# A fused state-space and gated-MLP layer: the state projection uses four PSUM banks in turn instead of two

## The chip, the core and the metric

The kernel runs on one NeuronCore of a Trainium2 chip. The core has five engines that run side by side, each through its own program in order, and wait for one another by semaphores: TensorE (PE in the profile; PEld is its weight load), VectorE (DVE), ScalarE (ACT), GpSimdE (POOL) and SyncE (SP), which here only issues DMAs. TensorE writes its products to PSUM, of which this kernel uses eight buffers ("banks") of 128 partitions by 512 float32 numbers. The metric is the time of one execution on the device in microseconds (us), the median over several runs.

## The reference

x has 2048 rows of 512 numbers. It is normalised (layer norm) to xn, and the output is x + A(xn) + B(xn):

```python
xn = _layernorm(x, axis=-1)
# A: a diagonal complex state-space layer with 512 states
Bu = jnp.einsum("bld,pd->blp", x + 0j, B_bar)
for t in range(L):
    h = Lam_bar[None, :] * h + Bu[:, t, :]
y = 2.0 * jnp.einsum("blp,dp->bld", hseq, Cmat).real + x * Dskip[None, None, :]
# B: a gated MLP with 1792 hidden units
h = _silu(gate) * up
out = jnp.einsum("bsf,fd->bsd", h, w2)
```

Here `x` inside A and B is xn. The state projection is the `Bu` product, in its real and its imaginary part; the factor that turns B into B_bar is applied elsewhere in the kernel (it is folded into C).

## The kernel before

The 2048 rows are cut into four blocks b = 0 to 3 of 512 rows (`TBLK`), and each block has these stages.

**Layer norm** gives `xn` (rows on partitions) and its transpose `xnT`. Block 0 is transposed on TensorE, the others by DMA. Block 1 is normalised by VectorE, blocks 2 and 3 by ScalarE (L269 sums, L275 squares, L285 the result); for block 3 the unneeded elementwise result of L269 and L275 goes to buffers of the `y_ps` pool.

**Gated MLP** (`glu(b)`, L512): for each of 14 slices f of 128 hidden units, four matmuls with w1 and four with w3 (L518, 128x512 each) fill two banks of the `gu_ps` pool, ScalarE reads them out with Silu (L527) and Copy (L528), and VectorE multiplies the two for pairs of slices (L536) into `act`.

**State projection** (`bu(b)`, L425): for two halves hf, two tiles j in a half and the real and imaginary part ri, eight groups of four matmuls each (L434). This text numbers the groups of a block 1 to 8. Each group accumulates in one bank, and ScalarE copies the bank to the tile `u` (L436, "eviction"). `u` has three buffers, one per half. A bank can be written again when its eviction is done, and a buffer of `u` when VectorE has finished with its former content. `bu(b)` stands inside `glu(b)` before slice 8, 8 and 4 for b = 0, 1, 2 (`AHEAD`), and for b = 3 it stands by itself after `glu(2)`.

**Scan** (`ssm_tasks(b)`, L442): VectorE rotates `u` (L456, L459, L463), runs eight scans along time (L473), rotates back (L479, L483), and GpSimdE issues a DMA that adds the last part into `act` (L487).

**Output product** (`y_fast(n)`, L701, n = 0 to 7, two for each block): a 256-row pair times the stacked weights in seven half-size products instead of eight (`mms`, L717, 128x256 matmuls). VectorE forms the sums of input tiles (L676, L759) and of results (L728), and ScalarE copies partial results from bank to bank (L737) and seeds banks (L698). The four result banks come from `gu_ps` or from two of `bu_ps` and two of `y_ps` (`seeds`, L682: `bu_ps` and `y_ps` for n = 0, 3, 4 and 6). The pair's rows are stored from `xn`.

PSUM has three pools: `ps_gu` with four banks, `ps_bu` with two and `ps_y` with two; a pool hands out its banks in turn. The order of work on each engine is written out by hand (`manual_schedule`): the code's order is the order of the engine's program. VectorE's work of the scan and of the weight sums is placed between the other work by `Filler` (L23), which counts assumed costs, not times that it measures: `bg.tensor(0.86)` after each projection group, for instance. Small ScalarE tasks (`sins`) are placed by `sin_step`, one at a time.

Around the later part of the kernel the order on TensorE is `y_fast(1)`, `glu(2)` with `bu(2)` in it, `bu(3)`, `y_fast(2)`, `y_fast(3)`, `glu(3)`, `y_fast(4)` to `y_fast(7)`.

Of the kernel before, what the change touches and what calls it, by code (L numbers as in the profile page):

```python
# [14 lines left out]
FP32 = DT.float32  # L15
BF16 = DT.bfloat16
FP16 = DT.float16
P = 128
# [45 lines left out]
def kernel(  # L64
# [22 lines left out]
    TBLK = CPB * P  # L87
# [31 lines left out]
    ps_bu = ctx.enter_context(tc.tile_pool(name="ps_bu", bufs=2, space=bass.MemoryType.PSUM))  # L119
    ps_y = ctx.enter_context(tc.tile_pool(name="ps_y", bufs=2, space=bass.MemoryType.PSUM))  # L120
# [214 lines left out]
    def sin_step(until=None):  # L335
        while sins and (until is None or until not in sins_done):
            key, fn = sins.popleft()
            fn()
            sins_done.add(key)
            if until is None:  # L340
                break
# [83 lines left out]
    def bu(b):  # L425
        for hf in range(NPT // 2):
            u = up.tile([P, 2, 2, TBLK], BF16, name="u")
            u_blk[b, hf] = u
            for j in range(2):
                pt = 2 * hf + j  # L430
                for ri in range(2):
                    ps = ps_bu.tile([P, TBLK], FP32, name="bu_ps")
                    for dt in range(NDT):
                        nc.tensor.matmul(out=ps, lhsT=bt[:, ri, dt, pt * P:(pt + 1) * P], rhs=xnT_blk[b][:, dt, :],  # L434
                                         start=(dt == 0), stop=(dt == NDT - 1))
                    nc.scalar.activation(out=u[:, j, ri, :], in_=ps, func=ACT.Copy)  # L436
                    bg.tensor(0.86)
                if (b == 0 and pt > 0) or (b == 1 and ri == 1) or (b == 2 and pt > 1):
                    sin_step()
            bg.fill()  # L440
# [71 lines left out]
    def glu(b):  # L512
# [77 lines left out]
        for f in range(f0, NFT):  # L590
            if f == AHEAD[b]:
                if b == 0:
                    ssm_tasks(0)
                bu(b)
            g_ps = ps_gu.tile([P, TBLK], FP32, name="gu_ps")
            mms(g_ps, w1_sb, f, slice(0, TBLK))
            u_ps = ps_gu.tile([P, TBLK], FP32, name="gu_ps")
            mms(u_ps, w3_sb, f, slice(0, TBLK))
            evac(f, g_ps, u_ps)
            if b in (1, NBLK - 1) and f == NFT - 3:  # L600
                seeds(0 if b == 1 else 4)
            if b == 0 and f == FIRST:
                sin_step((0, 0))
            elif b > 0 or f != MID - 1:
                sin_step()
            bg.tensor(1.72)
            bg.fill()
            if pend and f % 2 == 0:
                gate()
# [227 lines left out]
    sin_step(("ln", 3, True))  # L837
    seeds(2)
    bu(3)
    res_tasks(2)  # L840
    posts = ssm_tasks(3, True)
# [44 lines left out]
```

## Time and profile before

| | |
|---|---|
| median of 5 runs | 206.68 us (206.41 to 207.63) |
| the profiled execution's own time | 206.41 us |
| its span, from first to last instruction | 204.6 us |
| TensorE, matmul busy | 198.0 us (97%) |
| VectorE busy | 179.0 us (87%) |
| ScalarE busy | 125.1 us (61%) |
| GpSimdE busy | 35.0 us (17%) |
| projection matmuls (L434), 124 records | 28.9 us |
| projection evictions (L436), 32 | 18.8 us, 594 ns each |

A matmul's record lasts longer than its turn on the engine, because matmuls are pipelined: a 128x512 matmul is shown with 379 ns, but one starts every 216 ns (111 records fill the 24.00 us from 144 to 168). A wait shorter than the difference leaves no idle time in the record, and must be found from the starts. About one matmul record in fifty is missing from the trace. In lists of instructions in order of time, the columns are start, duration, engine, line, operation, tiles written and read, shapes, count, and in brackets the idle time before and what ended it. In the chain that ended last they are start, duration, and engine, tile and line.

### The profile page before, as it was taken

Reading aid. Unit: us, or ns where it says so; the run is one execution under the profiler, and the core shown is the slowest. Engines: PE = TensorE matmul, PEld = TensorE weight load, DVE = VectorE, ACT = ScalarE, POOL = GpSimd, SP = SyncE. Lnnn points to the kernel's source line nnn. Section 1 sums busy time; section 2 is a strip of 40 time slices with the busy share of each in tenths; the row PEclk is TensorE's granted clock in tenths of the full one; section 3 lists DMA queues with packets and bytes.
Section 4 is the critical chain, followed back from the end, with each engine's and each line's share of the span. In section 5 each row is a group of like instructions: output and inputs, shape, how many; then the busy total and the mean of one; then the engine's idle time right before and its main releaser. Section 6 shows DMA issues by size and latency. Waiting matters only on the chain.

```text
span 204.6 us, 3425 instructions
## 1 busy us (share of the span) xinstructions
PE 198.0 (97%) x1304; PEld 122.2 (60%) x1317; DVE 179.0 (87%) x248; ACT 125.1 (61%) x251; POOL 35.0 (17%) x59
## 2 busy tenths in 40 slices
PE   7999999999999999999999999999999999999994
PEld 2864444444444578854444444888444458888893
DVE  3789699999987999999969999997999998857932
ACT  4799788699999956689767775210566672101010
POOL 3250289500310040231010001011000011100000
PEclk9999999999999999999999999999999999999999
DMA  6899999993870002414660003219200037151011
GB/s 172 258 225 185 316 187 109 352 221 112 154 144 13 0 0 54 103 51 79 106 128 0 0 0 65 42 39 205 68 0 0 0 74 135 35 122 51 29 40 38
DMA packets 27832, 20.01 MB, mean 98 GB/s; under 512 B 15912, under 2 KB 26280, under 8 KB 27816
## 3 DMA queue, kind: packets, MB, share of 16 engines
q1 hardware_dynamic: 25512, 13.21, 28.1%
q0 software_dynamic: 1728, 6.29, 16.3%
q10 hardware_dynamic: 576, 0.30, 0.5%
q8 instruction: 10, 0.16, 0.4%
q14 instruction: 6, 0.05, 0.1%
HBM read 7.74 MB, written 2.10 MB: 48 GB/s over the span
## 4 chain that ended last, share of the span: by engine, by line
PE 45%; DVE 41%; ACT 5%; issue 4%; DMA 4%; POOL 1%; ACTq 0%; DVEq 0%
PE gu_ps L518 15%; PE gu_ps L717 11%; DVE u L473 7%; PE y_ps L717 7%; PE bu_ps L717 6%; DVE act L536 5%; PE bu_ps L434 4%; DVE p L456 3%; DVE u L459 3%; DMA xn<-x_blk 3%; DVE tw L655 2%; DVE u L463 2%; DVE stats L214 2%; DVE act L483 2%; DVE xn L728 2%
## 5 line engine op out<-in xcount | busy, mean ns | idle before, releaser
L518 PE MATMUL gu_ps<-xnT,w_sb 128*128 128x512 bf16 x415 | 92.0, 379 | 0.5
L518 PEld LDWEIGHTS <-w_sb 128*128 128x128 bf16 x424 | 41.4, 98 | 49.6 <-issue 0.3
L717 PEld LDWEIGHTS <-act 128*128 128x128 f16 x451 | 43.2, 98 | 6.3 <-DVE act L759 0.9
L527 ACT ACTIVATE g<-gu_ps 128x512 bf16<-128x512 f32 x55 | 33.0, 601 | 13.7 <-PE gu_ps L518 13.1
L528 ACT ACTIVATE u<-gu_ps 128x512 bf16<-128x512 f32 x55 | 33.2, 603 | 9.6 <-PE gu_ps L518 9.2
L434 PE MATMUL bu_ps<-xnT,bt 128*128 128x512 bf16 x124 | 28.9, 379 | 0.9 <-ACT u L436 0.4
L434 PEld LDWEIGHTS <-bt 128*128 128x128 bf16 x128 | 12.5, 98 | 16.7 <-issue 2.1
L436 ACT ACTIVATE u<-bu_ps 128x512 bf16<-128x512 f32 x32 | 18.8, 594 | 5.9 <-PE bu_ps L434 4.9
L473 DVE TENSOR_TENSOR_SCAN u<-rho,act,u 128x512 bf16<-128x512 f32 x16 | 19.5, 1265 | 0.0
L536 DVE TENSOR_TENSOR act<-g,u 128x1024 f16<-128x1024 bf16 x28 | 19.0, 678 | 0.3 <-ACT u L528 0.3
L487 POOL DMA_DIRECT2D act<-p x8 | 7.2, 898 | 65.3 <-DVE act L483 43.6
L456 DVE TENSOR_TENSOR p<-u,tabe 128x2048 bf16<-128x2048 bf16 x8 | 9.8, 1219 | 1.8 <-ACT g L527 1.6
L717 PE MATMUL y_ps<-tw,act 128*128 128x256 f16 x88 | 10.9, 273 | 0.0
L717 PE MATMUL gu_ps<-w_sb,act 128*128 128x256 bf16 (+1 forms) x84 | 10.8, 268 | 0.0
L717 PE MATMUL gu_ps<-tw,act 128*128 128x256 f16 x88 | 10.8, 273 | 0.0
L737 ACT ACTIVATE bu_ps<-y_ps 128x256 f32<-128x256 f32 x4 | 1.5, 369 | 13.7 <-PE y_ps L717 13.7
L459 DVE TENSOR_TENSOR u<-u,tabe 128x2048 bf16<-128x2048 bf16 x8 | 9.8, 1219 | 0.1
L479 DVE TENSOR_TENSOR p<-u,tabe 128x2048 f16<-128x2048 bf16 x8 | 9.8, 1220 | 0.1
L473 DVE TENSOR_TENSOR_SCAN u<-rho,ends,u 128x512 bf16<-128x512 f32 x8 | 9.8, 1264 | 0.0
L463 DVE TENSOR_TENSOR u<-u,p 128x2048 bf16<-128x2048 bf16 x8 | 9.7, 1216 | 0.1
L483 DVE TENSOR_TENSOR act<-u,tabe 128x2048 f16<-128x2048 bf16 x8 | 9.7, 1214 | 0.0
L717 PEld LDWEIGHTS <-tw 128*128 128x128 f16 x99 | 8.8, 98 | 0.9
(140 smaller groups left out, 253.7 us busy)
## 6 DMA issues: line engine op xcount, KB each, us to landing
act<-p POOLq DMA_DIRECT2D x8, 512.0 KB, 5.1
xn<-x_blk POOLq DMA_DIRECT2D x4, 512.0 KB, 5.6
out_dram<-xn SPq DMA_DIRECT2D x15, 128.0 KB, 1.7
w_sb<-in_B_w_dram SPq DMA_DIRECT2D x1, 1792.0 KB
x_blk<-in_A_x_dram SPq DMA_DIRECT2D x3, 512.0 KB, 11.8
w_sb<-in_B_w_dram SPq DMA_DIRECT2D x2, 768.0 KB, 7.3
w_sb<-in_B_w_dram SPq DMA_DIRECT2D x4, 256.0 KB, 3.7
w_sb<-in_B_w_dram SPq DMA_DIRECT2D x2, 512.0 KB, 7.1
```

What stands on the lines that cost most here:

```text
L434: nc.tensor.matmul(out=ps, lhsT=bt[:, ri, dt, pt * P:(pt + 1) * P], rhs=xnT_blk[b][:, dt, :], start=(dt == 0), stop=(dt == NDT - 1))
L436: nc.scalar.activation(out=u[:, j, ri, :], in_=ps, func=ACT.Copy)
L456: nc.vector.tensor_tensor(out=st["p"], in0=st["g"], in1=tabe[:, psl, 1:3, :], op=ALU.mult)
L459: nc.vector.tensor_tensor(out=st["g"], in0=st["g"], in1=tabe[:, psl, 0:1, :].to_broadcast(FULL), op=ALU.mult)
L463: nc.vector.tensor_tensor(out=st["g"], in0=st["g"], in1=st["p"][:, :, ::-1, :], op=ALU.subtract)
L473: nc.vector.tensor_tensor_scan(out=v, data0=rho[:, pt:pt + 1].to_broadcast([P, TBLK]), data1=v, initial=init, op0=ALU.mult, op1=ALU.add)
L483: nc.vector.tensor_tensor(out=act_state(b, hf), in0=st["g"], in1=tabe[:, psl, 0:1, :].to_broadcast(FULL), op=ALU.mult)
L518: nc.tensor.matmul(out=ps[:, tsl], lhsT=w[:, dt, f * P:(f + 1) * P], rhs=xnT[:, dt, tsl], start=(dt == 0), stop=(dt == NDT - 1))
L527: nc.scalar.activation(out=g16[:, f % 2, :], in_=g_ps, func=ACT.Silu)
L528: nc.scalar.activation(out=u16[:, f % 2, :], in_=u_ps, func=ACT.Copy)
L536: nc.vector.tensor_tensor(out=act(b)[:, k0:k1 + 1:k1 - k0, :], in0=g16, in1=u16, op=ALU.mult)
L717: nc.tensor.matmul(out=out, lhsT=left[:, k, :], rhs=right[k][:, cols], start=(start and k == 0), stop=(k == NK - 1), skip_group_check=True)
```

## The change

Of the eight projection groups of a block, those with j = 0 (groups 1, 2, 5, 6) still take a bank from `ps_bu`, and those with j = 1 (groups 3, 4, 7, 8) take one from `ps_y`. A group therefore reuses the bank of the group four before it, not two before it. Matmuls, evictions, assumed costs and the order of every engine's instructions are what they were. The lines after the first edited one move down by one.

```diff
             for j in range(2):
                 pt = 2 * hf + j
                 for ri in range(2):
-                    ps = ps_bu.tile([P, TBLK], FP32, name="bu_ps")
+                    pool, name = (ps_bu, "bu_ps") if j == 0 else (ps_y, "y_ps")
+                    ps = pool.tile([P, TBLK], FP32, name=name)
                     for dt in range(NDT):
                         nc.tensor.matmul(out=ps, lhsT=bt[:, ri, dt, pt * P:(pt + 1) * P], rhs=xnT_blk[b][:, dt, :],
                                          start=(dt == 0), stop=(dt == NDT - 1))
```

## The prediction

> **What bounds the kernel now.** I read the busy shares first, then the chain that ended last, then TensorE's waits, then the four projection stages in order of time. The busy shares name TensorE:
>
> ```profile
> PE 198.0 (97%) x1304; PEld 122.2 (60%) x1317; DVE 179.0 (87%) x248; ACT 125.1 (61%) x251; POOL 35.0 (17%) x59
> ```
>
> Busy matmul records overlap, so the share says where to look, not what is free. The chain says where TensorE sets the end:
>
> ```profile
> 89.29 0.34 DVE xn L728
> ...
> 95.65 0.70 ACT xn L285
> 96.34 0.50 ACT u L436
> 96.84 0.04 issue
> 96.88 2.53 PE bu_ps L434 x11
> ...
> 123.22 1.15 DVE act L483
> 124.37 0.02 issue
> 124.39 0.02 ACTq L436
> 124.41 0.04 issue
> 124.45 0.61 ACT u L436
> 125.06 0.04 issue
> 125.10 1.89 PE bu_ps L434 x8
> 126.99 8.41 PE gu_ps L717 x77
> ```
>
> The reader should see three things. VectorE holds the chain almost throughout until 89.6. From 125.10 it is TensorE without a break until 200.46, so a microsecond that TensorE gains there is a microsecond at the end, unless something else is late. And twice TensorE starts a projection matmul right after an eviction (L436), at 96.88 and 125.10: that is a wait for a bank. The second shows in the list in order of time:
>
> ```profile
> 119.33 5.34 PE L434 MATMUL bu_ps<-xnT,bt 128*128 128x512 bf16 x23
> 125.10 1.89 PE L434 MATMUL bu_ps<-xnT,bt 128*128 128x512 bf16 x8 [0.43 <-ACT u L436]
> 126.82 0.93 PE L717 MATMUL gu_ps<-w_sb,act 128*128 128x256 bf16 x7
> ```
>
> **The waits, block by block.** A stage of 32 matmuls at 0.216 us needs 6.92 us. From its first start to the first start of the next stage the trace has: bu(0) 21.17 to 28.29, 7.12 us; bu(1) 52.47 to 59.80, 7.33 us; bu(2) 94.85 to 102.06, 7.21 us; bu(3) 119.33 to 126.82, 7.49 us. The excess is 0.20, 0.41, 0.29 and 0.57 us, 1.47 us in all. In each case ScalarE is late: in bu(3) its eviction of group 5 waits 0.87 us for VectorE's L483 to free a `u` buffer, and group 7 needs group 5's bank; in bu(2) three L285 of 0.80 us and slice evictions stand before group 1's eviction (96.25 to 96.85), and group 3 needs that bank at 96.58.
>
> **The change, part by part.** Nothing is added to any engine's program and nothing moves past anything; only the bank differs. Evictions from `y_ps` should cost what those from `bu_ps` do: the nearest rows are 0.597 us for L239, a 128x512 read of `y_ps`, and 0.594 us for L436. The 16 moved evictions bring 16 x 0.003 = 0.05 us of ScalarE work either way, beside other work: zero.
>
> *bu(2).* Groups 3 and 4 find `y_ps` banks whose last users (L275, done at 89.1) are long gone, and group 5 needs group 1's eviction, which ends at 96.85, 1.5 us before group 5's turn at 94.85 + 4 x 0.865 = 98.31. So all 0.29 us go. From 102.06 to 119.33 TensorE does ten slices of eight matmuls, 80 x 0.216 = 17.3 us in 17.27 us: no wait in which to lose it. bu(3) then starts at 119.04. Bounds of the gain: 0 to 0.31 (96.88 minus the due 96.58, rounded); taken 0.29.
>
> *bu(3).* VectorE's L483 still ends at 124.36, because VectorE's chain from 107.21 hangs on its own work, not on TensorE. Group 5's eviction therefore still starts at 124.45 and group 6's follows at about 124.95. Groups 7 and 8 no longer ask for these: they need groups 3 and 4, evicted by 123.6. TensorE runs through and ends group 8's turn at 119.04 + 6.92 = 125.96 instead of 126.82. ScalarE evicts group 7 at about 125.5 and group 8 from 126.1 to 126.7; behind them stands the first L737 of y_fast(2), which needs its 11 matmuls (1.20 us, and 0.16 us of pipeline), so 127.3. It is covered by 0.6 us. Bounds of the gain: 0 to 0.58 (125.10 minus the due 119.33 + 6 x 0.865 = 124.52); taken 0.57.
>
> *What is late next.* y_fast(2) begins 0.86 us earlier. VectorE is where it could be caught:
>
> ```profile
> 129.11 1.22 DVE L479 TENSOR_TENSOR p<-u,tabe 128x2048 f16<-128x2048 bf16 x1
> 130.63 0.89 DVE L759 TENSOR_TENSOR act<-act,x_blk 128x1408 f16<-128x1408 f16 x1 [0.29 <-PE gu_ps L717]
> ...
> 139.03 0.89 DVE L759 TENSOR_TENSOR act<-act,tw 128x1408 f16<-128x1408 f16 x1 [0.66 <-PE bu_ps L717]
> ...
> 171.61 0.89 DVE L759 TENSOR_TENSOR act<-act,x_blk 128x1408 f16<-128x1408 f16 x1 [0.89 <-PE bu_ps L717]
> ```
>
> L759 waits for TensorE each time, so VectorE has little to give. At the first it moves up only by its idle 0.29, to 130.34, and ends at 131.23. The product that reads it starts at 132.83 now and would be due at 131.97: 0.74 us of cover, the smallest anywhere. At the second L759 both engines are 0.3 and 0.86 us early, the idle 0.66 shrinks to about 0.1, and the reader (141.23, due at 140.37) has 1.3 us. At the third VectorE is free at 170.42, TensorE's release comes at about 170.75, and the reader is due at 172.95, over 1.3 us later. The sum DMA of block 3 (L487, issued at 177.52, awaited until 183.00) hangs on VectorE work that TensorE's results release, so it moves along; its reader at 185.82 starts 1.9 us after the sum of 0.89 us made from it. The last adds and stores follow TensorE's end. If one of these covers fails, the gain shrinks by what it lacks, and no term here adds time.
>
> *bu(0) and bu(1).* TensorE would be up to 0.61 us earlier, but it then runs into VectorE:
>
> ```profile
> 75.96 0.88 DVE L759 TENSOR_TENSOR act<-act,x_blk 128x1408 f16<-128x1408 f16 x1
> 76.90 0.94 PE L717 MATMUL bu_ps<-w_sb,act 128*128 128x256 bf16 x7 [0.57 <-DVE act L759]
> ```
>
> VectorE goes from 26.3 to 76.8 with a single wait over 0.2 us, 2.19 us for a DMA that its own L615 triggered. I take 0: the earlier TensorE waits that much longer at 76.90. Bounds of the gain: 0 to 0.61.
>
> **The sum.** 0.29 + 0.57 = 0.86 us, against the profiled execution's own 206.41 (span 204.6 and 1.8 around it) 205.55. That execution is 0.27 us below the median of the five, 206.68, so the median is predicted at 205.82.
>
> **A rule against it.** The granted clock is 1.00 in each stretch that I asked for, the four projection stages with their waits and the solid stretch from 103 to 119 (15.95 of 16.00 us busy) among them. The Trainium skill, "TensorE: Matmul & The Clock Gate", section "A second HAM failure mode: psum-queue depth-cycling", reports a kernel whose 512-column bf16 matmuls cycled through PSUM banks and made the clock oscillate between half and full rate; its window of about 3.4 us at half rate would cost an estimated 1.7 us, 207.5 in all. I go by the row, in which banks are cycled already.
>
> **The rivals.**
> 1. *Only bu(3) pays.* If the 0.29 us of bu(2) are lost before 119.33, to a ScalarE queue that is late elsewhere, 206.68 - 0.57 = 206.11. Against it: no wait in 80 matmuls.
> 2. *VectorE takes the wait over.* If L759 at 130.6 or its followers lack their cover, up to all 0.86 us go and the time is 206.7. For it: the idle of 0.29 us; against it: 0.74 us of cover beyond.
> 3. *All four stages pay*, if VectorE's chain before 76.8 moves up with TensorE: 206.68 - 1.47 = 205.21. Only its shared waits could do that.
> 4. *Slower: block 3's sum DMA is late.* From issue (L487 at 177.52) to use (L676 at 183.00) it takes 5.48 us and has 1.93 us of cover; longer by that plus 0.86 us it eats the gain, by 0.62 us more, from 8.9 us on, the kernel is slower. The trace's slow row for 512 KB is the load of x, 11.8 us to landing: 206.68 - 0.86 + (11.8 - 5.48 - 1.93) = 210.2. For it: stores of finished rows run beside it, and all of them shift. Against it: they shift together, the same kind of transfer took 4.93 us (136.54 to 141.47), and from 168 to 204 the DMA engines are 0.30 busy on average.
> 5. *The banks were not what it waited for*, and the starts at 96.88 and 125.10 only coincide with evictions: 206.68. Against it: start and eviction end lie 0.04 us apart both times.
>
> **How the numbers follow.** The forecast has 0.67, the rivals 0.11, 0.09, 0.04, 0.05 and 0.04. The forecast's own range is 205.6 to 206.05. From rival 3's 205.2 to no gain at 206.7, only rival 4 falls outside, so that is the range. About 0.3%, 0.62 us, is what a measurement of this kernel can tell from no change, so faster means below 206.06: the forecast and rival 3 with little loss, 0.70. Within it: rivals 1, 2, 5, 0.23. Slower: rival 4 and what I have not thought of, 0.07.
>
> **What would show it.** Right: the first starts of bu(2)'s and bu(3)'s next stages come 6.92 us after their own; no idle time of L434 behind L436 at bu(3); ScalarE's wait for L483 there still 0.9 us or more; L759 at 130.3 without a wait; the idle before 76.90 grown from 0.57 to about 1.2 us. Wrong: a new TensorE wait between 126 and 200, on L759 or a DMA, or a granted clock below 1.00.

## The result and the profile after

The changed kernel takes 205.85 us (median of 43 runs, 204.75 to 206.87), the kernel before, on the same chips, 206.79 us (85 runs). The ratio is 0.9952 with a 95% interval of 0.994 to 0.9964: 0.99 us less, between 0.74 and 1.24. Ratios here and below leave out runs in a slower state (in the experiments one, with bu(2) alone, 210.04 us), and they are not the quotients of the medians beside them, from which they differ by up to 0.2%. The prediction was 205.82 us. The profiled execution took 205.53 us, 0.88 us less than the profiled execution before (206.41); its span is 203.8 us.

The page's first part shows that the engines' work is what it was to within 0.3 us, but for GpSimdE's 36.0 us instead of 35.0:

```profile
span 203.8 us, 3425 instructions
PE 197.7 (97%) x1304; PEld 122.5 (60%) x1317; DVE 179.0 (88%) x248; ACT 124.9 (61%) x251; POOL 36.0 (18%) x59
```

So the gain must lie in waits. TensorE's waits in the changed kernel (waiting engine, tile and line, what it waited for; then us in total, times, longest):

```profile
PE bu_ps L718 <- DVE act L760: 1.2, 1, 1.2
PE bu_ps L193 <- PEq L871: 0.8, 1, 0.8
PE bu_ps L551 <- DMA w_sb<-in_B_w_dram: 0.3, 1, 0.3
```

The wait of bu(3) for a bank (L434 behind L436, 0.43 us of idle time in the profile before) is gone. The wait for VectorE's L759, now L760, has grown from 0.57 to 1.21 us of idle time. This idle time also follows a wait of VectorE for a DMA, which ends at 62.8 us and whose length differs between executions (last section). Where that wait was nearly the same, 2.05 to 2.20 us, the idle time was 0.57 us with two banks in bu(0) and bu(1) (the profile before, and bu(3) alone below) and 1.21 and 1.30 us with four (this profile, and bu(0) and bu(1) alone below), so the growth is not an accident of two executions. The other two lie in the first 9 us, ahead of the first projection. In order of time on TensorE, bu(3) now is:

```profile
119.06 1.67 PE L435 MATMUL bu_ps<-xnT,bt 128*128 128x512 bf16 x7
120.79 1.89 PE L435 MATMUL y_ps<-xnT,bt 128*128 128x512 bf16 x8
122.51 1.89 PE L435 MATMUL bu_ps<-xnT,bt 128*128 128x512 bf16 x8
124.24 1.89 PE L435 MATMUL y_ps<-xnT,bt 128*128 128x512 bf16 x8
125.97 0.93 PE L718 MATMUL gu_ps<-w_sb,act 128*128 128x256 bf16 x7
```

The starts lie 1.73, 1.72, 1.73 and 1.73 us apart, which is eight matmuls at 0.216: there is no wait, not even one short enough to hide in the overlap of the records. All four stages now take 6.91 us from their first start to the next stage's (before: 7.12, 7.33, 7.21 and 7.49).

**Where the time went.** Both executions have one instant that VectorE and not TensorE sets: the first product after the wait for L759. It starts at 76.903 before and at 76.940 after. From there to the first matmul of y_fast(2) it is 49.92 us before and 49.03 after, 0.89 us less. From y_fast(2) to TensorE's last matmul nothing more is gained or lost: that one starts at 201.43 before and 200.57 after, 0.86 us apart.

### The profile page after: what moved, and what is told of

It reads as the page before. It is cut to its first block, busy times and chain, and to the rows that moved or that the text cites. A ratio compares the mean times of both kernels' runs of the same rounds, so it can differ in the third digit from the quotient of the medians.

```text
span 203.8 us, 3425 instructions
## 1 busy us (share of the span) xinstructions
PE 197.7 (97%) x1304; PEld 122.5 (60%) x1317; DVE 179.0 (88%) x248; ACT 124.9 (61%) x251; POOL 36.0 (18%) x59
## 4 chain that ended last, share of the span: by engine, by line
PE 54%; DVE 32%; DMA 5%; issue 3%; ACT 2%; SPq 2%; POOL 1%; DVEq 0%
PE gu_ps L519 23%; PE gu_ps L718 12%; PE y_ps L718 7%; PE bu_ps L718 6%; DVE u L474 5%; DVE act L537 4%; PE y_ps L435 3%; PE bu_ps L435 3%; DMA xn<-x_blk 3%; DVE tw L656 2%; DVE p L457 2%; DVE u L460 2%; DMA w_sb<-in_B_w_dram 2%; DVE xn L729 2%; DVE ct L397 1%
## 5 line engine op out<-in xcount | busy, mean ns | idle before, releaser
L435 PE MATMUL y_ps<-xnT,bt 128*128 128x512 bf16 x63 | 15.1, 379 | 0.1
L435 PE MATMUL bu_ps<-xnT,bt 128*128 128x512 bf16 x61 | 14.8, 379 | 0.1
L437 ACT ACTIVATE u<-bu_ps 128x512 bf16<-128x512 f32 x16 | 9.3, 594 | 2.6 <-PE bu_ps L435 2.2
L437 ACT ACTIVATE u<-y_ps 128x512 bf16<-128x512 f32 x16 | 9.5, 595 | 1.9 <-PE y_ps L435 1.3
```

## The experiments

The edits change the condition in the first changed line, or what is shown. Shares of a stage are starts compared with starts, as above; ratios are to the kernel before on the same chip.

### One stage at a time

**bu(3) alone**

```diff
-                    ps = ps_bu.tile([P, TBLK], FP32, name="bu_ps")
+                    pool, name = (ps_bu, "bu_ps") if j == 0 or b != 3 else (ps_y, "y_ps")
+                    ps = pool.tile([P, TBLK], FP32, name=name)
```

> The four banks in bu(3) alone. My theory: its wait of 0.57 us goes and nothing else, so 0.57 us faster than before, about 206.2 against 206.8 (ratio 0.9972); bu(2) keeps its 0.29 us, y_fast(2) starts at about 126.25 in the profile. If the whole gain of the change came from bu(3), 0.86 us (0.9958); if the banks were not what TensorE waited for, no change.

Measured: 205.98 us against 207.01, ratio 0.9954 (0.9933 to 0.9975). The interval holds the expected 0.9972, but also the whole gain of the changed kernel, so the trace has to tell them apart. bu(3) takes 6.91 us, bu(2) keeps its 7.21 with a bank wait of 0.31 us in it, and from the product behind L760 (76.707) to y_fast(2) (126.044) it is 49.34 us, 0.58 less than before. The term of 0.57 us is there, alone.

**bu(2) alone**

```diff
+                    pool, name = (ps_bu, "bu_ps") if j == 0 or b != 2 else (ps_y, "y_ps")
```

> The four banks in bu(2) alone. My theory: bu(3) starts 0.29 us earlier, but there the bank of group 5 comes free when VectorE's L483 lets its eviction go, at a time that TensorE does not move, so TensorE's wait in bu(3) grows from 0.57 to 0.86 us (idle shown 0.43 to 0.72) and the time is that of before, 206.8. If the terms simply added, 0.29 us faster (0.9986), 206.5.

Measured: 206.95 us against 207.01, ratio 0.9994 (0.9968 to 1.002). bu(2) takes 6.91 us and has no wait, yet nothing is gained. TensorE in order of time, in bu(3) of this kernel:

```profile
120.54 5.34 PE L435 MATMUL bu_ps<-xnT,bt 128*128 128x512 bf16 x23
126.57 1.89 PE L435 MATMUL bu_ps<-xnT,bt 128*128 128x512 bf16 x8 [0.69 <-ACT u L437]
128.29 0.93 PE L718 MATMUL gu_ps<-w_sb,act 128*128 128x256 bf16 x7
```

TensorE comes to bu(3) 0.3 us earlier and waits 0.69 us instead of 0.43 for the same eviction; the stage takes 7.76 us instead of 7.49. From the product behind L760 (78.411 in this execution) to y_fast(2) it is 49.88 us, 0.04 less than before. The eviction hangs on VectorE's L484, and VectorE did not move: from the start of its L760 near 77 us to the end of that L484 it is 48.36 us, before 48.40.

**bu(0) and bu(1) alone**

```diff
+                    pool, name = (ps_bu, "bu_ps") if j == 0 or b > 1 else (ps_y, "y_ps")
```

> The four banks in bu(0) and bu(1) alone. My theory: TensorE is 0.61 us earlier up to 76.3 and then waits for VectorE's L759, which ends at the same time as before; the idle time ahead of that product grows from 0.57 to about 1.2 us and the time stays at 206.8. If VectorE's work before 76.8 moves up with TensorE, up to 0.61 us faster (0.9970), 206.2.

Measured: 206.88 us against 207.01, ratio 0.9981 (0.9959 to 1.0004), which holds no change and leaves out the changed kernel's 0.9952. Both stages take 6.91 us, and the wait behind L760 is where their gain is spent (0.64 us in the traces: 7.12 and 7.33 become 6.91):

```profile
77.21 0.94 PE L718 MATMUL bu_ps<-w_sb,act 128*128 128x256 bf16 x7 [1.29 <-DVE act L760]
```

From start to start the extra there is 1.46 us, before it was 0.74. That is 0.72 us more: the gain of 0.64, and 0.08 us by which VectorE's L760 comes later after bu(0)'s first start in this execution. After it bu(2) takes 7.21, bu(3) 7.50 us, and from 77.212 to y_fast(2) it is 49.93 us, as before.

**bu(2) and bu(3) together**

```diff
+                    pool, name = (ps_bu, "bu_ps") if j == 0 or b < 2 else (ps_y, "y_ps")
```

> The four banks in bu(2) and bu(3), two banks in bu(0) and bu(1). My theory: all of the change's gain, 0.86 us below before (0.9958), because bu(2) pays as soon as bu(3) does not wait; y_fast(2) starts 49.06 us after the product that waits for L759 near 76.9, as in the changed kernel (125.97 - 76.94 = 49.03). If bu(0) and bu(1) carried part of it, less.

Measured: 205.69 us against 207.30, ratio 0.9936 (0.991 to 0.9963). bu(0) and bu(1) keep 7.12 and 7.34 us, bu(2) and bu(3) take 6.91, and from the product behind L760 (78.275) to y_fast(2) (127.307) it is 49.03 us, the changed kernel's own number. These two stages are the whole effect. Their worth is 0.58 (bu(3) alone), 0.04 (bu(2) alone) and 0.89 us (both): bu(2)'s part pays only behind a bu(3) that doesn't wait.

### The cause of bu(3)'s wait, removed without another bank

The kernel before with its two banks, but the second half of block 3 is evicted into a buffer that nothing else holds by then, so ScalarE needn't wait for L483:

```diff
-            u = up.tile([P, 2, 2, TBLK], BF16, name="u")
+            if b == 3 and hf == 1:
+                u = xtp.tile([P, NDT, TBLK], BF16, name="xnT").rearrange("p (j r) t -> p j r t", r=2)
+            else:
+                u = up.tile([P, 2, 2, TBLK], BF16, name="u")
```

> Two banks as before, but the second half of bu(3) puts its u into a buffer that is free by then (that of block 2's xnT), so its eviction does not wait for VectorE's L483. My theory: the late eviction, not the number of banks, is the cause of the wait; the 0.87 us wait of ScalarE and the 0.43 us idle of TensorE are gone with two banks, 0.57 us faster than before (0.9972), 206.2, the same as four banks in bu(3) alone. If two banks are too few by themselves, TensorE still waits in bu(3) and the time stays within 0.1 us of before.

Measured: 206.29 us against 207.01, ratio 0.9966 (0.9946 to 0.9987). TensorE in bu(3) of this kernel, in order of time, and ScalarE's eviction of group 5:

```profile
122.27 7.07 PE L437 MATMUL bu_ps<-xnT,bt 128*128 128x512 bf16 x31
129.17 0.93 PE L720 MATMUL gu_ps<-w_sb,act 128*128 128x256 bf16 x7
```

```profile
126.78 0.60 ACT L439 ACTIVATE xnT<-bu_ps 128x512 bf16<-128x512 f32 x1 [0.27 <-PE bu_ps L437]
```

With two banks and no late eviction the stage takes 6.91 us. From bu(2)'s first start to y_fast(2)'s it is 31.385 us, before 31.973: 0.59 gained. So two banks are enough for eight groups in turn; what was missing was one eviction, held up by a buffer of `u`. The change doesn't remove that lateness, it gives TensorE two banks to go on with while ScalarE waits. In the changed kernel ScalarE still waits as long, and longer:

```profile
124.46 1.08 ACT L437 ACTIVATE u<-bu_ps 128x512 bf16<-128x512 f32 x2 [1.15 <-PE bu_ps L435]
125.43 1.34 ACT L437 ACTIVATE u<-y_ps 128x512 bf16<-128x512 f32 x2
127.43 0.37 ACT L738 ACTIVATE gu_ps<-gu_ps 128x256 f32<-128x256 f32 x1 [0.66 <-PE gu_ps L718]
```

The profile puts the 1.15 us down to the matmuls, but group 5's last matmul starts at 122.51 + 3 x 0.216 = 123.16 and its record of 0.38 us ends at 123.54; VectorE's L484 ends at 124.36, and it is L484 that releases the eviction. Before, the same eviction began at 124.45.

Why does L484 end so late? VectorE's work up to it starts behind a wait of 1.6 us. Before, and in the changed kernel:

```profile
107.21 1.22 DVE L456 TENSOR_TENSOR p<-u,tabe 128x2048 bf16<-128x2048 bf16 x1 [1.63 <-ACT g L527]
```

```profile
107.22 1.23 DVE L457 TENSOR_TENSOR p<-u,tabe 128x2048 bf16<-128x2048 bf16 x1 [1.60 <-DMA act<-p]
```

The profile before puts this wait down to ScalarE's L527, which follows TensorE. But in all twelve profiles of this text the line starts 0.09 us after the landing of a DMA `act<-p` (L487; issued at 102.55 and landed at 107.12 before, 102.58 and 107.12 after). That DMA reads one of the two buffers of `p`, and L456 is about to write it. So VectorE, and with it the late eviction, waits here for a DMA and not for TensorE, which is why an earlier TensorE does not bring L483 forward. Whether a third buffer of `p` would free bu(3) with two banks was not tried.

### How much cover VectorE has left

The prediction said that L759 of y_fast(2) could end 0.74 us later before TensorE felt it, and named it the smallest cover anywhere. Into the changed kernel one multiplication is put ahead of that line, whose result is not used, once with 1024 columns and once with 2048:

```diff
+        if n == 2:
+            spare = xtp.tile([P, NDT, TBLK], BF16, name="xnT").rearrange("p k t -> p (k t)")
+            nc.vector.tensor_tensor(out=spare[:, 0:2048], in0=x_blk[2].rearrange("p c d -> p (c d)")[:, 0:2048],
+                                    in1=x_blk[3].rearrange("p c d -> p (c d)")[:, 0:2048], op=ALU.mult)
         nc.vector.tensor_tensor(out=v["s4"], in0=v["a12"], in1=v["s2"], op=ALU.subtract)
```

> The changed kernel with one added VectorE product of 128x1024 (0.68 us alone, 0.60 from start to start) ahead of L759 in y_fast(2); its result is not used. My theory: the product that reads L759's result has 0.74 us of cover there by the prediction, 0.8 by the trace after, so L759 ends about 131.75 against 131.97 due and TensorE does not wait: the time stays that of the changed kernel, about 0.4% below before (0.9952). If VectorE already carries the end there (the rival in which VectorE takes the wait over), 0.6 us slower than the changed kernel (0.998).

> The same with a product of 128x2048 (1.22 us alone, 1.14 from start to start). My theory: the cover is exceeded by 1.14 - 0.8 = 0.3 to 0.4 us, TensorE waits that long for L759 near 132, and the time is 0.35 us above the changed kernel's (ratio to before 0.997). With no cover 1.1 us above (1.0007), with a wide one 0.

Measured: with 1024 columns 206.21 us, ratio 0.9949 (0.9922 to 0.9977), with 2048 columns 206.10 us, ratio 0.9982 (0.996 to 1.0005), both against 206.86. The intervals are as wide as the effect, and the two medians do not even stand in the order of the ratios; the traces decide. With 1024 columns L764 (the former L759) starts 0.60 us after the added line and TensorE reads its result without a wait, at the turn that is due. With 2048 columns, VectorE and then TensorE:

```profile
130.35 1.22 DVE L762 TENSOR_TENSOR xnT<-x_blk 128x2048 bf16<-128x2048 bf16 x1
131.49 0.89 DVE L764 TENSOR_TENSOR act<-act,x_blk 128x1408 f16<-128x1408 f16 x1
```

```profile
132.43 0.94 PE L718 MATMUL gu_ps<-w_sb,act 128*128 128x256 bf16 x7 [0.20 <-DVE act L764]
```

The added line delays L764 by 1.14 us (130.35 to 131.49). TensorE's start comes 0.365 us later than its pace would have it. So 1.14 - 0.365 us of the delay, about 0.78, cost nothing: that is the cover, where 0.74 was predicted.

### Taking away what swallowed bu(0) and bu(1)

In the changed kernel 1.37 us of TensorE's time are lost at 76.94, to a VectorE that at 60.8 had begun to wait 2.05 us for a DMA (2.19 in the kernel before; ahead of the third of the first pair's sums of input tiles, L676, which overwrites the tile `x_blk` that the DMA reads). VectorE has four L397 behind that sum which don't need the DMA. In both kernels the sum is moved behind them:

```diff
-    for t in row_sums(0, *pairs[0]):
+    sums0 = row_sums(0, *pairs[0])
+    for t in sums0[:2]:
         bg.add(*t)
     for fn in finish_c[2:]:
         bg.add(1.4, fn, "tw")
+    bg.add(*sums0[2])
```

**In the kernel before, with two banks**

> The kernel before, two banks, with the third sum of the first pair (L676, which waits 2.19 us for a DMA at 60.6) moved behind the four L397, so that VectorE works in that time. My theory: VectorE is up to 2.1 us earlier from 63 on, TensorE's waits at 76.90 (0.74 from start to start) and 89.67 (0.23) go, and L483 releases group 5 of bu(3) early enough that its 0.57 us go as well, with two banks: 0.74 + 0.23 + 0.57 = 1.5 us faster than before (0.9926). If VectorE's order there does not matter, no change.

Measured: 205.63 us against 206.86, ratio 0.9944 (0.9927 to 0.9962): 1.16 us (0.79 to 1.51), where 1.5 was expected; from bu(0)'s first start to y_fast(2)'s the traces have 105.65 us before and 104.62 here, 1.03 less. TensorE's wait behind L759 and one of 0.2 us later are gone, but bu(3) still has 0.52 us. TensorE, then ScalarE:

```profile
124.83 1.89 PE L434 MATMUL bu_ps<-xnT,bt 128*128 128x512 bf16 x8 [0.36 <-ACT u L436]
```

```profile
124.18 1.09 ACT L436 ACTIVATE u<-bu_ps 128x512 bf16<-128x512 f32 x2 [0.81 <-DVE act L483]
```

I had expected that VectorE would keep all of its new lead until L483. It did not: in y_fast(0) and y_fast(1) it now waits for TensorE's products.

```profile
74.73 0.89 DVE L759 TENSOR_TENSOR act<-act,x_blk 128x1408 f16<-128x1408 f16 x1 [0.21 <-PE bu_ps L717]
...
83.14 0.89 DVE L759 TENSOR_TENSOR act<-act,tw 128x1408 f16<-128x1408 f16 x1 [0.66 <-PE gu_ps L717]
```

From there VectorE is as far ahead of TensorE as TensorE allows: from the start of this second L759 to the end of L483 it takes 40.95 us, before 40.81. So L483 is late for bu(3) by nearly what it was.

**In the changed kernel, with four banks**

> The changed kernel, four banks, with the same move. My theory: nothing hides the gain of bu(0) and bu(1) any more, so TensorE loses neither the 1.37 us that it waits at 76.94 in the changed kernel nor the 0.23 us at 89.71: 1.6 us faster than the changed kernel, 2.4 us faster than before (0.988), and 0.9 us (0.20 + 0.41 + 0.29) faster than the same move with two banks. If the bank waits of bu(0) and bu(1) are lost elsewhere, only 0.3 us faster than the move with two banks.

Measured: 204.03 us (203.84 to 204.5) against 206.86, ratio 0.9871 (0.9854 to 0.9888). A second series of the same program:

> The kernel of reorder4 once more, next to the others. By the first run 0.987 of before; 0.989 if only the computed 2.4 us are there.

It gave 204.15 us (203.78 to 204.98) against 207.30, ratio 0.9857 (0.9829 to 0.9886). VectorE around the moved sum:

```profile
60.50 2.73 DVE L397 SCALAR_TENSOR_TENSOR ct<-ct,w2c,tw 128x512 f16<-128x512 bf16 x4
63.45 0.89 DVE L677 TENSOR_TENSOR x_blk<-x_blk,act 128x1408 f16<-128x1408 f16 x1 [0.22 <-DMA xn<-x_blk]
```

The wait for the DMA is 0.22 us instead of 2.19, with the four L397 in its place. TensorE's only waits left, the whole list:

```profile
PE bu_ps L193 <- PEq L873: 0.8, 1, 0.8
PE y_ps L238 <- DVE xn L219: 0.2, 1, 0.2
```

Both lie in the first 6 us. In this order of work the four banks are worth all four stages. From bu(0)'s first start to y_fast(2)'s, which leaves the start-up out, two banks take 104.62 us (21.94 to 126.56) and four 103.15 (21.12 to 124.27): 1.47 us. The excess of the four stages with two banks is 0.21 + 0.43 + 0.31 + 0.52 = 1.47. The medians of the two kernels on one chip, 205.63 and 204.03, say 1.6. This is the version to keep. From bu(0)'s first start to y_fast(2)'s it is 1.60 us faster than the change alone (104.75 to 103.15); its two ratios divided by the changed kernel's 0.9952, which comes from runs on more chips, are 0.9919 and 0.9905, which would be 1.7 and 2.0 us.

## Why the prediction was right

*bu(2) 0.29 and bu(3) 0.57 us, summed to 0.86.* Right in time (0.89 in the traces; 0.74 to 1.24 by the runs) and in place: y_fast(2) was to start at 125.96 and starts at 125.97. The stages need 6.906 us and not 6.92, so the terms are 0.31 and 0.59. That the median came within 0.03 us of the forecast is partly luck: the forecast started from a median of 206.68 over five runs, the 85 runs have 206.79, and the changed kernel's runs spread over 2.12 us. That bu(2)'s first eviction is late because of the L285 ahead of it was read from the trace and not tried. What the working left out is that the two terms are not independent. It costed bu(2) by its own wait and checked only that the 17.27 us after it hold no stall. For bu(2) alone the same working would have said 0.29, and the trace says 0.04: the earlier start is handed to the wait for group 5's eviction, which VectorE pins. The sum came out because the change removes both.

*bu(0) and bu(1) worth nothing.* Right: their gain went into the wait behind L759, idle 1.21 us against about 1.2 predicted. The agreement to 0.01 us needed an execution with nearly the same DMA wait (2.05 us, before 2.19); others had 1.03 to 1.51 us with four banks there. The bound of "0 to 0.61" was a real one; the moved sum opened it.

*Two banks wait for L483, not for the matmuls.* Right: a free buffer of `u` removes the wait without a third bank. Group 5's eviction was to start at 124.45 still, and starts at 124.46; the evictions from `y_ps` take 0.60 us as those from `bu_ps` do, so their predicted cost of zero stands. That TensorE does not move L483 was right, but the prediction took VectorE's work from 107.21 on as given and passed over the 1.63 us wait at its head, which its profile put down to ScalarE's L527 behind TensorE; it is the DMA `act<-p` that holds it.

*What is late next.* The four lines of VectorE that the prediction followed, in the changed kernel:

```profile
129.12 1.23 DVE L480 TENSOR_TENSOR p<-u,tabe 128x2048 f16<-128x2048 bf16 x1
130.27 0.88 DVE L760 TENSOR_TENSOR act<-act,x_blk 128x1408 f16<-128x1408 f16 x1
...
138.18 0.89 DVE L760 TENSOR_TENSOR act<-act,tw 128x1408 f16<-128x1408 f16 x1 [0.24 <-PE bu_ps L718]
...
170.75 0.89 DVE L760 TENSOR_TENSOR act<-act,x_blk 128x1408 f16<-128x1408 f16 x1 [0.22 <-PE bu_ps L718]
...
182.18 0.89 DVE L677 TENSOR_TENSOR x_blk<-act 128x1408 f16<-128x1408 f16 x1 [1.39 <-DMA act<-p]
```

The first L760 starts at 130.27 without a wait (130.34 predicted), the second waits 0.24 us (about 0.1), the third starts at 170.75 (170.75). L677, which waits for block 3's sum DMA, starts at 182.18, 0.82 us earlier than before.

*The rivals.* Rival 1 (only bu(3) pays, ratio 0.9972) and rival 3 (all four, 0.9929) lie outside the interval, and the traces show which stages pay. Rival 2 (VectorE takes the wait over) would have needed the cover of L760 gone; it is 0.78 us after the change. Rival 4 fell: block 3's sum DMA was issued 0.86 us earlier, at 176.66, and took 5.43 us to its landing, before 5.39. Rival 5 fell with the missing waits.

*The rule weighed against the trace.* The granted clock reads 1.00 in the three stretches of the changed kernel that hold bu(1), bu(2) and bu(3) (52 to 60, 94 to 102, 119 to 126), and TensorE is busy for 22.84 of their 23.00 us. What the Trainium skill, "TensorE: Matmul & The Clock Gate", section "A second HAM failure mode: psum-queue depth-cycling", reports of another kernel does not show in these stages, nor in the four with two banks (1.00 as well, by the prediction's windows).

## What to carry to other kernels

Price a wait for a PSUM bank as the stage's length, first start to next stage's first start, minus matmuls times their spacing; here the four stages lost 1.5 us with two banks, of which the page counts 0.9 us as idle time of L434 and the list of waits names 0.4. Then follow the instant that the stage's end hands on: a gain counts only if no later wait is pinned by an engine that the gain doesn't move, and where one is (bu(0) and bu(1) before L759, bu(2) before bu(3)'s late eviction), it only lengthens that wait until the pin is removed too. More banks cover a late eviction and do not make it earlier, so look for what holds the eviction up, and for work that can fill another engine's wait for a DMA.

## What the runs showed of the hardware

**How long VectorE waits for the DMA from `x_blk` to `xn` varies from one execution to the next**, and TensorE feels it. The nine profiles with the third sum in its first place have 1.90 to 3.71 us, with 4.96 to 6.66 us from the DMA's issue to its landing. In five of them all the code ahead is the same: 2.19 us in the profile before, 2.20 with four banks in bu(3) alone, 2.82 in bu(2) alone, 3.71 in both, and 3.70 with the free `u` buffer:

```profile
64.32 0.89 DVE L679 TENSOR_TENSOR x_blk<-x_blk,act 128x1408 f16<-128x1408 f16 x1 [3.70 <-DMA xn<-x_blk]
```

TensorE then stood idle for 1.99 us behind L762, until 78.40. With the sum moved, the runs spread over 0.66 and 1.20 us with four banks (4 and 6 runs) and over 1.66 us with two (11 runs), against 2.12 us for the changed kernel (43 runs). A few runs reach less far than many by chance too, so that the DMA makes a difference there was not shown.

**After that idle time the clock halved once.** The windows of the same execution (window; its length; busy us of PE, PEld, DVE, ACT and POOL, with instructions; granted clock of TensorE; DMA share; GB/s):

```profile
78.00:80.00 2.00, 1.60 (x9) 1.21 (x10) 1.97 (x5) 1.57 (x3) 0.40 (x1) 0.65 0.00 0
80.00:82.00 2.00, 2.00 (x11) 1.41 (x10) 2.00 (x4) 1.36 (x2) 0.00 (x0) 0.50 1.27 70
82.00:84.00 2.00, 2.00 (x20) 1.77 (x18) 2.00 (x5) 0.12 (x1) 0.00 (x0) 0.99 0.37 70
```

From 78.62 to 82.03, 3.41 us, the granted clock was 0.50; a 128x256 matmul started every 0.213 us instead of every 0.109, so about 1.7 us were lost. Of these, 1.44 us are still lost at bu(2)'s first start. They, the longer wait for the DMA (the product behind L762 starts 1.5 us later after bu(0)'s first start than in the profile before) and bu(2)'s 0.3 us are why that execution's span is 207.0 us, 3.2 more than the changed kernel's, although its bu(3) stage is as short. The Trainium skill, "TensorE: Matmul & The Clock Gate", section "HAM oscillation — how this bites in real kernels", warns of idle gaps above about 3.4 us; here one of 1.99 us was followed by the drop, while idle times of 1.99 us (bu(2) and bu(3) together) and 1.87 us (bu(2) alone), in other executions, were not: there the clock stayed at 1.00. What decides between them was not tried. Such a drop need not be rare: 3.41 us at half rate lower the mean clock of a run of 207 us to 0.992, and three of the 80 runs of the kernel before that are listed with the experiments have that clock, with 209.01, 209.02 and 209.32 us, as has one of bu(2) alone (210.04 us). None of the 43 runs of the changed kernel has it, so that its longer wait behind L760 brings such drops is not shown.
